# Router logits with their operands swapped, a last eviction shared by two engines, a drain moved, and a new order planned with later landings

## The chip, the cores and the metric

The kernel runs on one core of one Trainium2 chip. The metric is the device time of one execution in microseconds (us), the median of several executions. The core has five engines with queues of their own, each worked off in order: TensorE (PE; its weight loads are shown as PEld), VectorE (DVE), ScalarE (ACT), GpSimd (POOL) and SyncE (SP), which here issues nearly all transfers. The indirect gathers and scatters are issued by GpSimd.

## The reference

Three blocks follow one another.

1. Attention over 32 memories for 4 batches, 8 heads, 576 positions, 64 wide. `a` is the softmax of `phi` over the positions; `k_m` and `v_m` are the sums of k and v weighted with `a`; the scores of q against `k_m` go through a softmax over the 32 memories and weigh `v_m`.
2. A gated layer on 2304 tokens of 512: `silu(x @ w_gate) * (x @ w_val) @ w_out`, 1536 wide.
3. A mixture of 8 experts with one expert a token:

```
logits = x @ w_gate                      # 2304 x 8
expert_idx = argmax(logits)
gate_w = softmax(logits)[expert_idx]
h = relu(disp @ w1[e]);  y = h @ w2[e]   # 512 -> 1024 -> 512
out[i] = gate_w[i] * y[expert_idx[i], pos[i]]
```

A token is kept while its expert has counted fewer than `capacity` tokens before it.

## The kernel before

Matmuls run on pairs of fp32r tiles: a value is cut into a rounded high part and the rest (`cut`, L430 and L432: a ScalarE copy, then a subtraction on VectorE or GpSimd), and three of the four products of parts are summed.

Batches 0 and 1 are the first pair, 2 and 3 the second. Per batch, `phi` is turned and the memories are formed (L523, L545), turned again (L584), and q is multiplied with them for the scores (L632), whose softmax runs on VectorE, GpSimd and ScalarE. `memories_in` projects the memories through the gate and value weights (pm, L838), and the result is cut into mh on ScalarE and VectorE. `batch` multiplies it with the attention weights (pg, pv, L940); `gates` applies silu. `products` multiplies with the output weights (py, L984), in three groups G of four 128-wide slices. The weights are converted once on chip, stored in DRAM, and reloaded for the second pair (L807).

After the third group each chunk of 128 tokens leaves as `rows`. `rows_out` turns it with four transposes (pw, L1033), cuts it into yh, and multiplies it with the router weights rg, 16 columns (8 experts, high and low parts), in eight matmuls (pl, L1043). There are 18 chunks. `route` takes three at a time, six blocks in all: it copies pl from 16 partitions to SBUF (lt, L1082, ScalarE), turns it back with three transposes so that tokens stand on partitions (L1086), and computes the choice, the position and the gate with some thirty small VectorE instructions.

The experts run as units of up to 288 tokens. A unit's index list feeds three indirect gathers (L1452, GpSimd), the rows are turned (L1473), and `up` and `down` multiply with the expert's w1 and w2 (L1500, L1540). The weights come in eight transfers of 512 KB a unit and are cut on ScalarE and VectorE (`part1`, `part2`). Each quarter of the result is copied out (y, L1555, ScalarE), turned (po, L1566), scaled with the gate on VectorE (L1579) and scattered to the output (L289, GpSimd). Two early units need only the first pair, six come later, then one unit of 128 tokens (class `Small`), whose result is scaled in one VectorE instruction (L1733) and scattered last. A GpSimd drain (L1639) stands behind the gather of this last unit.

No engine chooses its order at run time. A planner, `Loom`, runs in Python while the program is built. Every piece of work is a generator that says which engine it needs next, for how long, and which events and buffers it waits for; the planner keeps a clock for each engine and takes the waiting piece with the lowest rank among those that could start. The ranks are the numbers in `RANK`, added to due times. A transfer is given a time of landing, `loom.landed`: one after another at 410 KB a us, and 0.75 us on top. Instructions go into each engine's queue in the order that the planner comes to them. On the chip each waits for its semaphores only, but it holds everything behind it on its engine.

Of the kernel before, what the change touches and what calls it, by code (L numbers as in the profile page):

```python
# [21 lines left out]
RANK = {  # L22
    "gate": -318.1, "mh": -66.7, "mem": -464.3, "mem0": 36.2, "py": 408.0, "out": -17.0, "tables": 252.9, "warm": -9,
# [5 lines left out]
    "mh1": -406.0, "py1": 7.4, "turn": -21.0, "route": -340.6, "zeros": -518.5, "lists": -509.6, "marks": -304.6, "pick": -568.4,  # L29
# [149 lines left out]
def on_pe(count, n=288, passes=1):  # L179
    return "PE", count * (passes * n / 2400 + 0.011)  # L180
# [18 lines left out]
def attention_moe_moe_kernel(  # L199
# [60 lines left out]
    def t2k(shape, name, dt=F32):  # L260
        return sb.tile(shape, dt, tag="t2k", name=name, bufs=4)
# [172 lines left out]
    class Attention:  # L434
# [12 lines left out]
        def load(self):  # L447
            b = self.b
            if b >= 2:
                for Q in range(2):  # L450
                    yield atts[b - 1].kvq[Q][1]
            yield raw_s
            self.ph = traw([128, 2, S], "ph")
            loom.set(self.ph_in)
            for Q in range(2):
                yield on_dma(295)
                nc.sync.dma_start(self.ph[:, Q], phi[b, Q])
                loom.set(self.phq[Q], loom.landed)
# [7 lines left out]
        def load_kv(self, Q):  # L466
            slot = self.kv_slot(Q)
            if slot is not raw_s:
                for hp in range(2):
                    yield slot  # L470
            else:
                yield self.ph_in
                yield pair
                for hp in range(2):
                    yield raw_s
                loom.put(pair)
            for hp in range(2):
                raw = self.raws[Q][hp] = kvraw(self.b, Q).rearrange("p (t h) j d -> p t h j d", t=2)
                yield on_dma(655)
                nc.sync.dma_start(raw, kv[self.b, Q, hp])  # L480
                loom.set(self.kvq[Q][hp], loom.landed)
# [4 lines left out]
        def load_q(self, n):  # L486
# [20 lines left out]
            loom.set(self.qq[n], loom.landed)  # L507
# [285 lines left out]
    def reload(key, k):  # L793
# [15 lines left out]
        loom.set(wdone[1, key], loom.landed)  # L809
# [207 lines left out]
    def rows_out(P, py, rows, k):  # L1017
# [23 lines left out]
        for d in range(NDT):  # L1041
            for a in range(2):
                nc.tensor.matmul(  # L1043
                    pl[: 2 * E, c * TC : (c + 1) * TC],
                    rg[:, d].rearrange("p a e -> p (a e)"),
                    yh[:, a, d * TC : (d + 1) * TC],
                    start=(d == 0 and a == 0),
                    stop=(d == NDT - 1 and a == 1),
                )
# [24 lines left out]
    def route(blk):  # L1074
# [4 lines left out]
        yield t2k_s  # L1079
        lt = t2k([2 * E, RB * TC], "lt")  # L1080
        yield on_a(RB * TC)
        nc.scalar.copy(lt, pl[: 2 * E, : RB * TC])  # L1082
        px = pl[:, RB * TC :]
        yield on_pe(RB, 130)
        for c in range(RB):
            nc.tensor.transpose(  # L1086
                px[:, c * 2 * E : (c + 1) * 2 * E], lt[:, c * TC : (c + 1) * TC], ident[: 2 * E, : 2 * E]
            )
        loom.put(t2k_s)
        lg2 = small([TC, RB, 2, E], "lg2")  # L1090
        yield on_v(48)
        nc.vector.tensor_copy(lg2, px[:, : RB * 2 * E].rearrange("p (c a e) -> p c a e", a=2, e=E))
# [30 lines left out]
        pp = pl[:, RB * TC + 64 :]  # L1123
# [255 lines left out]
    class Unit:  # L1379
# [19 lines left out]
        def loads(self):  # L1399
# [4 lines left out]
            for d in range(NDT):  # L1404
# [5 lines left out]
                loom.spawn(self.part1(d, raw), self.base - 8 + d + RANK["w1"], loom.landed)  # L1410
            for t in range(NF2 // 2):
# [7 lines left out]
                loom.spawn(self.part2(t, raw), self.base + 8 + t + RANK["w2"], loom.landed)  # L1419
# [133 lines left out]
        def column(self, d, p2, y2):  # L1553
# [19 lines left out]
            for c in range(NC):  # L1573
# [17 lines left out]
                if c % 2 or c == NC - 1:  # L1591
                    loom.put(raw_s)
            loom.put(gw_s)
# [5 lines left out]
    class Small(Unit):  # L1599
# [20 lines left out]
        def gather(self):  # L1620
# [18 lines left out]
            nc.gpsimd.drain()  # L1639
# [69 lines left out]

        def down(self):  # L1710
            yield self.base + 6 + RANK["down"]
# [20 lines left out]
            yield on_v(DM)  # L1732
            nc.vector.tensor_scalar(ot, p2, self.gw, None, ALU.mult)  # L1733
# [122 lines left out]
```

## Time and profile before

| | us |
|---|---|
| median of three runs | 693.19 (692.75 to 693.77) |
| profiled execution, its own time | 699.14 |
| its span, first to last instruction | 697.4 |
| TensorE matmuls busy | 658.2 |
| VectorE, ScalarE, GpSimd busy | 407.9, 388.9, 232.2 |
| mean granted TensorE clock | 0.978 |

The durations all come from the one profiled execution, 5.95 us slower than the median of the runs. Busy times of a TensorE row overlap: matmuls are pipelined, and what one costs is read from the distance between starts, not from its own duration. In rows of the order of time, the number in brackets is the idle time of the engine before the instruction, with what ended it. The granted clock is given as a share: 1.00 is 2.4 GHz, 0.5 is 1.2 GHz, and a number between is a mean over a stretch with both.

### The profile page before, as it was taken

The numbers are of one execution on the slowest core, as the hardware profiler recorded it, in microseconds if no ns is written. First come the engines' busy times: TensorE is split into PE (matmuls) and PEld (weight loads), VectorE is DVE, ScalarE is ACT, GpSimd is POOL, SyncE is SP. The second block draws the span as 40 slices with busy tenths as digits, with TensorE's granted clock in tenths as the row PEclk, the third lists the DMA queues.
The fourth block names the chain that finished last, engine by engine and source line by source line (L and its number), as shares of the span: only waits on it lengthen the run. The fifth ranks groups of instructions, "written<-read, shape, count | busy, mean of one in ns | idle before, by whom it ended". The sixth has DMA issues, their size and how long they took to land. (4 is left out here: it accounts for less than half of the span.)

```text
span 697.4 us, 12482 instructions
## 1 busy us (share of the span) xinstructions
PE 658.2 (94%) x4681; PEld 604.5 (87%) x4681; DVE 407.9 (58%) x899; ACT 388.9 (56%) x735; POOL 232.2 (33%) x230
## 2 busy tenths in 40 slices
PE   6699999999898999999999999999999999999995
PEld 5489998988787788889988988898998999999983
DVE  3887744867566567603634646864573754754552
ACT  4779998986666356725713733434364544643450
POOL 1657654534434302511401320023461521321202
PEclk9699999999989999999999999999999999999997
DMA  9995768767743215794331432343964846655251
GB/s 349 402 378 194 257 229 297 288 220 253 293 175 133 89 57 195 265 290 143 128 121 37 176 105 107 107 123 88 259 205 140 274 123 205 198 152 203 85 192 36
DMA packets 48736, 132.03 MB, mean 189 GB/s; under 512 B 7648, under 2 KB 16864, under 8 KB 44064
## 3 DMA queue, kind: packets, MB, share of 16 engines
q1 hardware_dynamic: 45440, 121.44, 50.7%
q0 software_dynamic: 3232, 9.74, 4.2%
q8 instruction: 39, 0.64, 0.4%
q14 instruction: 25, 0.20, 0.1%
HBM read 98.10 MB, written 33.33 MB: 188 GB/s over the span
## 5 line engine op out<-in xcount | busy, mean ns | idle before, releaser
L984 PE MATMUL py<-wo,gh 128*128 128x512 f32 x648 | 156.7, 393 | 0.0
L984 PEld LDWEIGHTS py<-wo,gh 128*128 128x128 f32 x648 | 118.8, 188 | 23.3 <-ACT gh L430 0.2
L432 POOL TENSOR_TENSOR gh<-sg,gh 128x288 fp32r<-128x288 f32 x96 | 78.9, 826 | 151.6 <-ACT gh L430 151.1
L1540 PE MATMUL p<-hh,w2h 128*128 128x288 f32 x768 | 113.9, 299 | 0.0
L1500 PE MATMUL p<-xt,w1h 128*128 128x288 f32 x768 | 110.5, 297 | 0.0
L1540 PEld LDWEIGHTS p<-hh,w2h 128*128 128x128 f32 x768 | 104.3, 189 | 0.3 <-DVE hh L1516 0.2
L1500 PEld LDWEIGHTS p<-xt,w1h 128*128 128x128 f32 x768 | 104.0, 188 | 0.3 <-DVE yh L432 0.2
L289 POOL DMA_INDIRECT out_dram<-ot,idx x24 | 48.9, 2036 | 146.7 <-DVE ot L1579 143.7
L940 PE MATMUL pg<-at,mh 128*128 128x288 f32 x576 | 95.3, 303 | 2.3 <-DVE mh L432 1.2
L940 PE MATMUL pv<-at,mh 128*128 128x288 f32 x576 | 92.7, 298 | 0.9 <-ACT sg L850 0.9
L940 PEld LDWEIGHTS pg<-at,mh 128*128 128x128 f32 x576 | 82.9, 191 | 7.6 <-issue 2.3
L940 PEld LDWEIGHTS pv<-at,mh 128*128 128x128 f32 x576 | 82.1, 190 | 2.4 <-ACT sg L850 1.4
L853 DVE SCALAR_TENSOR_TENSOR sg<-sg,pv 128x288 f32<-128x288 f32 x96 | 43.1, 452 | 63.7 <-ACT sg L850 39.4
L432 DVE TENSOR_TENSOR mh<-pm,mh 64x512 fp32r<-64x512 f32 (+1 forms) x88 | 60.4, 686 | 18.5 <-ACT mh L430 16.2
L1514 ACT ACTIVATE hh<-p 128x288 fp32r<-128x288 f32 x64 | 26.2, 410 | 69.0 <-PE p L1500 60.7
L1516 DVE SCALAR_TENSOR_TENSOR hh<-p,hh 128x288 fp32r<-128x288 f32 x64 | 28.6, 450 | 56.0 <-ACT hh L1514 55.1
L430 ACT ACTIVATE mh<-pm 64x512 fp32r<-64x512 f32 (+1 forms) x88 | 51.9, 591 | 14.3 <-PE pv L940 9.2
L432 DVE TENSOR_TENSOR w2h<-w2r,w2h 128x1024 fp32r<-128x1024 f32 x34 | 41.3, 1216 | 28.2 <-ACT w2h L430 27.9
L430 ACT ACTIVATE gh<-sg 128x288 fp32r<-128x288 f32 x96 | 42.0, 441 | 26.8 <-DVE sg L853 25.5
L850 ACT ACTIVATE sg<-pg 128x288 f32<-128x288 f32 x96 | 38.6, 407 | 28.8 <-PE pg L940 26.1
L838 PE MATMUL pm<-wgv,tv 128*128 128x256 f32 x336 | 50.3, 301 | 4.3 <-DVE mh L432 2.2
L838 PEld LDWEIGHTS pm<-wgv,tv 128*128 128x128 f32 x336 | 46.9, 207 | 7.3 <-DVE mh L432 2.6
(215 smaller groups left out, 838.2 us busy)
## 6 DMA issues: line engine op xcount, KB each, us to landing
w1r<-in_moe_w_dram SPq DMA_DIRECT2D x36, 512.0 KB
w2r<-in_moe_w_dram SPq DMA_DIRECT2D x36, 512.0 KB
wr<-in_moe_w_gv_dram SPq DMA_DIRECT2D x24, 512.0 KB
wsc<-wgv SPq DMA_DIRECT2D x12, 1024.0 KB
wgv<-wsc SPq DMA_DIRECT2D x12, 1024.0 KB
kvraw<-in_kv_dram SPq DMA_DIRECT2D x16, 640.0 KB
wr<-in_moe_w_out_dram SPq DMA_DIRECT2D x12, 512.0 KB
osc<-wo SPq DMA_DIRECT2D x6, 1024.0 KB
```

Of the source, the lines that this page charges most:

```text
L289: ins = nc.gpsimd.indirect_dma_start(*args, **kwargs)
L430: nc.scalar.activation(hi, src, AF.Copy)
L432: (nc.gpsimd if pool else nc.vector).tensor_sub(lo, src, hi.bitcast(F32))
L838: nc.tensor.matmul(pm[:, Q * 256 : (Q + 1) * 256], tv[:, 2 * Q + hp, a, :], w[:, c, 2 * Q + hp], start=(k == 0 and n3 == 0), stop=(k == le ...
L850: nc.scalar.activation(sg, pg[:, :NB], AF.Silu, scale=1.0 / 256)
L853: nc.vector.scalar_tensor_tensor(sg, sg, 2.0**-16, pv[:, :NB], ALU.mult, ALU.mult)
L940: nc.tensor.matmul(pg[:, :NB], mh[:, a, Q, gv * 128 : gv * 128 + 128], at[:, Q, c, ns], start=(Q == 0 and n3 == 0), stop=(Q == 1 and n3 == 2),
L984: nc.tensor.matmul(py, gh[:, a, k * TC : (k + 1) * TC], wtiles[P, ws[j // 2]][:, j % 2, c, :], start=(j == 0 and n3 == 0), stop=(j == FG - ...
L1500: nc.tensor.matmul(p1[:, :NB], self.w1[d][:, a, f * 128 : f * 128 + 128], self.xt[d][:, c], start=(d == 0 and n3 == 0), stop=(d == NDT - 1 ...
L1514: nc.scalar.activation(dst[:, 0], p1[:, :NB], AF.Relu)
L1516: nc.vector.scalar_tensor_tensor(dst[:, 1], p1[:, :NB], 0.0, dst[:, 0].bitcast(F32), ALU.max, ALU.subtract)
L1540: nc.tensor.matmul(p2[:, :NB], self.w2[f // 2][:, f % 2, a, d * 128 : d * 128 + 128], self.hh[f][:, c], start=(f == 0 and n3 == 0), stop=( ...
```

## The change

- Logits: stationary and moving operand are swapped. Now yh (128 columns) is loaded and rg (16 columns) streams, so that the result has tokens on partitions. The copy lt and the transposes back are gone from `route`, with their buffer; the rest of `route` reads pl at other columns.
- `Small.down`: the last eviction is done half by ScalarE (new function `half`), half by VectorE; the scatter waits for both.
- The drain moves from behind the last unit's gather to behind the scatters of unit 6 of 0 to 7.
- The planner takes the loads of phi, kv and q of batches 2 and 3 and the reloads of converted weights to land 1.0 us later, and the experts' weights 1.5 us later.
- All ranks are new, and two settings of the planner: `slack` 0.02 to 0.01 and `look` 5.0 to 4.9.

```diff
-    "gate": -318.1, "mh": -66.7, "mem": -464.3, "mem0": 36.2, "py": 408.0, "out": -17.0, "tables": 252.9, "warm": -9,
+    "gate": -511.5, "mh": -86.7, "mem": -582.5, "mem0": -16.4, "py": 288.4, "out": -483.7, "tables": 87.1, "warm": -9,
...
-                loom.set(self.phq[Q], loom.landed)
+                loom.set(self.phq[Q], loom.landed + (1.0 if self.b >= 2 else 0.0))
...
-                loom.set(self.kvq[Q][hp], loom.landed)
+                loom.set(self.kvq[Q][hp], loom.landed + (1.0 if self.b >= 2 else 0.0))
...
-            loom.set(self.qq[n], loom.landed)
+            loom.set(self.qq[n], loom.landed + (1.0 if self.b >= 2 else 0.0))
...
-        loom.set(wdone[1, key], loom.landed)
+        loom.set(wdone[1, key], loom.landed + 1.0)
...
                 nc.tensor.matmul(
-                    pl[: 2 * E, c * TC : (c + 1) * TC],
+                    pl[:, c * 2 * E : (c + 1) * 2 * E],
+                    yh[:, a, d * TC : (d + 1) * TC],
                     rg[:, d].rearrange("p a e -> p (a e)"),
-                    yh[:, a, d * TC : (d + 1) * TC],
...
-        yield t2k_s
-        lt = t2k([2 * E, RB * TC], "lt")
-        yield on_a(RB * TC)
-        nc.scalar.copy(lt, pl[: 2 * E, : RB * TC])
-        px = pl[:, RB * TC :]
-        yield on_pe(RB, 130)
-        for c in range(RB):
-            nc.tensor.transpose(
-                px[:, c * 2 * E : (c + 1) * 2 * E], lt[:, c * TC : (c + 1) * TC], ident[: 2 * E, : 2 * E]
-            )
-        loom.put(t2k_s)
...
-        nc.vector.tensor_copy(lg2, px[:, : RB * 2 * E].rearrange("p (c a e) -> p c a e", a=2, e=E))
+        nc.vector.tensor_copy(lg2, pl[:, : RB * 2 * E].rearrange("p (c a e) -> p c a e", a=2, e=E))
...
-                loom.spawn(self.part1(d, raw), self.base - 8 + d + RANK["w1"], loom.landed)
+                loom.spawn(self.part1(d, raw), self.base - 8 + d + RANK["w1"], loom.landed + 1.5)
...
-                loom.spawn(self.part2(t, raw), self.base + 8 + t + RANK["w2"], loom.landed)
+                loom.spawn(self.part2(t, raw), self.base + 8 + t + RANK["w2"], loom.landed + 1.5)
...
+            if self.n == NEARLY + NSTAT - 2:
+                nc.gpsimd.drain()
             loom.put(gw_s)
...
-            nc.gpsimd.drain()
...
+        def half(self, dst, src):
+            yield on_a(DM // 2)
+            nc.scalar.activation(dst, src, AF.Copy, scale=self.gw)
+            loom.set(self.halved)
...
-            yield on_v(DM)
-            nc.vector.tensor_scalar(ot, p2, self.gw, None, ALU.mult)
+            h = DM // 2
+            loom.spawn(self.half(ot[:, :h], p2[:, :h]), self.rank_of_end)
+            yield on_v(h)
+            nc.vector.tensor_scalar(ot[:, h:], p2[:, h:], self.gw, None, ALU.mult)
+            yield self.halved
```

## Rows read from the trace of the kernel before

**Rows 1.** The page's busy times: us, share of the span, instructions.

```profile
PE 658.2 (94%) x4681; PEld 604.5 (87%) x4681; DVE 407.9 (58%) x899; ACT 388.9 (56%) x735; POOL 232.2 (33%) x230
```

**Rows 2.** Stage table: length, busy time by engine, granted clock, DMA share, GB/s.

```profile
0.00:40.00 40.00, 27.16 (x224) 21.77 (x225) 26.09 (x61) 25.89 (x51) 15.77 (x21) 0.83 0.97 381
...
188.00:224.00 36.00, 29.34 (x184) 26.43 (x183) 22.13 (x42) 23.38 (x45) 17.73 (x18) 0.86 0.44 176
224.00:300.00 76.00, 73.27 (x509) 63.66 (x509) 50.14 (x172) 42.21 (x77) 24.63 (x27) 1.00 0.46 158
...
470.00:662.00 192.00, 186.85 (x1439) 185.34 (x1437) 106.84 (x161) 90.99 (x160) 60.69 (x37) 1.00 0.57 176
662.00:697.40 35.40, 25.90 (x142) 21.74 (x142) 13.80 (x14) 11.06 (x15) 5.60 (x5) 0.90 0.32 117
```

**Rows 3.** TensorE in order of time, 188 to 224: start, length, what.

```profile
191.89 2.13 PE L632 MATMUL psc<-qt,tk 128*64 128x288 f32 x8 [2.93 <-DMA qt<-in_q_dram]
...
203.80 0.54 PE L940 MATMUL pg<-at,mh 128*128 128x288 f32 x2 [0.71 <-ACT mh L430]
...
209.61 1.19 PE L632 MATMUL psc<-qt,tk 128*64 128x288 f32 x8
...
219.56 1.65 PE L838 MATMUL pm<-wgv,tv 128*128 128x256 f32 x6 [2.21 <-DVE mh L432]
```

**Rows 4.** SyncE's queue in order of time: the issue of that q.

```profile
183.33 0.33 SPq L506 DMA_DIRECT2D qt<-in_q_dram  x1
```

**Rows 5.** Stage table behind the first hole.

```profile
193.90:198.20 4.30, 4.30 (x31) 4.24 (x30) 2.12 (x6) 2.27 (x6) 1.16 (x1) 0.82 0.38 160
```

**Rows 6.** TensorE in order of time, around routing blocks at 247 and 436.

```profile
246.90 0.18 PE L1126 MATMUL pl<-ohb,tri 128*128 128x8 bf16 x1
...
246.98 0.17 PE L1129 MATMUL pl<-ohb,onesb 128*128 128x8 bf16 x1
...
435.95 0.35 PE L1086 MATMUL pl<-ident,lt 16*128 16x16 f32 x3
436.23 0.65 PE L1043 MATMUL pl<-yh,rg 128*16 128x128 f32 x8
436.73 1.04 PE L1033 MATMUL pw<-ident,rows 128*128 128x128 f32 x8
```

**Rows 7.** Two lines' weight loads: shortest, median, longest ns; first and last start.

```profile
L1043 PEld LDWEIGHTS pl<-yh,rg x144: 92/95/100, 231.0 to 445.0; 128*16 128x16 f32 x144
...
L940 PEld LDWEIGHTS pg<-at,mh x576: 186/188/333, 36.6 to 403.1; 128*128 128x128 f32 x192
```

**Rows 8.** Groups by line: the copy in `route`; busy us, mean ns, idle.

```profile
L1082 ACT COPY lt<-pl 16x384 f32<-16x384 f32 x6 | 2.8, 466 | 11.6 <-PE pl L1043 11.6
```

**Rows 9.** The line of the drain: ns, start.

```profile
L1639 POOLq DRAIN  x1: 6924/6924/6924, 577.5 to 577.5; - x1
```

**Rows 10.** GpSimd in order of time: the last large unit's first scatter.

```profile
682.08 0.92 POOL L289 DMA_INDIRECT out_dram<-ot,idx  x1 [18.26 <-DVE ot L1579]
```

**Rows 11.** Groups by line, shapes apart: evictions of 256 and 512 columns.

```profile
L1022 DVE TENSOR_TENSOR rows<-py,yp 128x256 f32<-128x256 f32 x4 | 1.5, 420 | 3.4 <-PE py L984 3.4
L1011 ACT COPY yp<-py 128x256 f32<-128x256 f32 x4 | 1.4, 378 | 3.0 <-PE py L984 3.0
...
L1733 DVE TENSOR_SCALAR ot<-p,gw_s 128x512 f32<-128x512 f32 x1 | 0.8, 751 | 3.6 <-PE p L1721 3.6
```

**Rows 12.** TensorE and ScalarE in order of time, around 493 and 665.

```profile
492.74 1.06 ACT L430 ACTIVATE w1h<-w1r 128x1024 fp32r<-128x1024 f32 x1 [1.60 <-DMA w1r<-in_moe_w_dram]
...
494.14 0.53 PE L1566 MATMUL po<-ident,y 128*96 128x128 f32 x3 [0.99 <-ACT y L1555]
...
664.30 1.06 ACT L430 ACTIVATE w1h<-w1r 128x1024 fp32r<-128x1024 f32 x1 [1.26 <-DVE w1h L432]
...
665.70 0.53 PE L1566 MATMUL po<-ident,y 128*96 128x128 f32 x3 [1.63 <-ACT y L1555]
```

**Rows 13.** Groups by line: the transposes of a unit's result; idle before them.

```profile
L1566 PE MATMUL po<-ident,y 128*96 128x128 f32 x96 | 15.9, 275 | 6.4 <-ACT y L1555 4.7 <-issue 1.7
```

More of the change, by code (lines that the diff above doesn't have):

```diff
@@ L22 @@
 RANK = {
-    "gate": -318.1, "mh": -66.7, "mem": -464.3, "mem0": 36.2, "py": 408.0, "out": -17.0, "tables": 252.9, "warm": -9,
[5 rows of a table removed]
-    "mh1": -406.0, "py1": 7.4, "turn": -21.0, "route": -340.6, "zeros": -518.5, "lists": -509.6, "marks": -304.6, "pick": -568.4,
[3 rows of a table removed]
+    "gate": -511.5, "mh": -86.7, "mem": -582.5, "mem0": -16.4, "py": 288.4, "out": -483.7, "tables": 87.1, "warm": -9,
[5 rows of a table added]
+    "mh1": -518.0, "py1": 86.7, "turn": -430.3, "route": 181.9, "zeros": -31.3, "lists": -569.1, "marks": -465.0, "pick": -422.3,
[3 rows of a table added]
 }
@@ L1122, in route @@
         nc.vector.tensor_copy(ohj, ohb[:, 2 * RB - 1].unsqueeze(2).to_broadcast([TC, E, JU]))
-        pp = pl[:, RB * TC + 64 :]
+        pp = pl[:, 64:]
         flat = ohb.rearrange("p c e -> p (c e)")
@@ L1708, in hidden @@
                 loom.set(self.h_ready[f])
+        def half(self, dst, src):
+            yield on_a(DM // 2)
+            nc.scalar.activation(dst, src, AF.Copy, scale=self.gw)
+            loom.set(self.halved)
         def down(self):
-            yield self.base + 6 + RANK["down"]
+            self.rank_of_end, self.halved = self.base + 6 + RANK["down"], Event()
+            yield self.rank_of_end
             yield self.h_ready[0]
```

16 rows, old and new, of the table RANK are left out of this document.

## The prediction

> **What bounds the kernel now.** I read four views in this order: the busy times, the stage table, TensorE's order of time in two stages, and the groups by line. TensorE does matmuls for 658.2 of 697.4 us [rows 1], so only what touches its queue counts, and the reader is to see in the stage table where it does not run. In 0 to 40 it lacks 12.8 us at a clock of 0.83, with the DMA engines 97% taken; in 188 to 224 6.7 us at 0.86; in 224 to 300 2.7; in 470 to 662 5.2; in the last stretch 9.5, mostly after its last product [rows 2]. Between the two bad stages, and from 300 to 430, nothing is to be had but fewer TensorE instructions. The rest of the engines are at 56 to 58% or less and matter by the order of their queues.
>
> In 188 to 224 there are three kinds of hole. At 191.89 the scores of the second pair waited 2.93 us for q, issued at 183.33: 8.6 us for 576 KB. At 203.80 and 219.56 products waited 0.71 and 2.21 us for cuts of mh on ScalarE and VectorE [rows 3, 4]. Each hole is followed by work at the lower clock: eight score matmuls take 2.13 us after the first hole and 1.19 us at 209.61 [rows 3], and 193.9 to 198.2 runs at a mean of 0.82 [rows 5]. With 1.00 for 2.4 GHz and 0.5 for 1.2 GHz, a mean of 0.86 over 36 us is 5.0 us of full-speed work lost. So this stage holds 6.7 + 5.0 = 11.7 us.
>
> **Router logits.** The 144 logits products swap operands: 16 columns of weights under 128 moving ones become 128 columns of weights (yh) under 16 moving ones. Now eight of them occupy 0.50 us (436.23 to 436.73), 62 ns each, set by the 128 moving columns, and their 16-column loads take 95 ns in the record; an fp32r load of 128 columns takes 188 ns [rows 6, 7]. The difference, 93 ns for 112 columns, is 0.83 ns a column, so 128 columns need 106 ns of loading. Under 288 moving columns that hides; under 16 there is nothing to hide it but the next load. Eight take 0.85 us, 0.35 more than now, and 18 groups 6.3 us more. Removed are 18 transposes in six groups of three, 0.28 us each (435.95 to 436.23), 1.7 us [rows 6]. Net +4.6 us, on the path, since these groups stand at 228 to 268 and 424 to 445, where TensorE has almost no idle time [rows 2]. Lower end: loads as quick as the bf16 ones, four starts in 0.08 us, 27 ns each [rows 6], give 18 x (0.22 - 0.50) - 1.7 = -6.8 us. Upper end: 188 ns each with no overlap, 18 x (1.50 - 0.50) - 1.7 = +16.4. The transposes removed also had 128-column loads under 16 columns, at 93 ns; that would be +2.7. I take 106 because it is worked out from loads of the same type and shape.
>
> The Trainium skill ("TensorE: Matmul & The Clock Gate", section "LDWEIGHTS (loading the stationary operand)") says that a load costs its columns divided by 1.2 per ns, whatever the rows, which speaks against this edit: 107 ns for 128 columns, and a sum of +4.7 us as an estimate from that page. The trace's 0.83 ns a column agrees; that the load then sets the pitch is shown by no row here.
>
> The six copies of lt on ScalarE (466 ns each, 2.8 us) go too [rows 8]. ScalarE is 56% busy and off the path there: nothing. The routing chain gets shorter by a copy and a transpose, but its end feeds gathers for units that come behind the two early ones, and TensorE has their work meanwhile: nothing. Should the cover be gone, one hop of about 0.5 us a block would show, 3 us.
>
> **Drain.** It lasted 6.92 us on GpSimd [rows 9]. It moves behind the scatters of the seventh unit, the last but one of the large ones, after which GpSimd stood idle for 18.26 us until 682.08 [rows 10]. Behind it wait the last unit's three scatters; 18.26 - 6.92 leaves 11 us. Nothing. If that idle time shrank below 6.92, each us less would delay the tail by one.
>
> **Last rows.** 512 columns on VectorE took 751 ns; 256 columns take 420 on VectorE and 378 on ScalarE, side by side [rows 11]. This is on the path: only the scatter and the end of the program follow. ScalarE has nothing left to do then. Gain 0.33 us; at best 0.37, and a loss of up to 0.2 if ScalarE wakes that much later.
>
> **Later landings and the new order.** These change no instruction but the order on every queue, and with it which wait is met. The second pair's loads are priced 1.0 us later, the experts' rows 1.5, reloads 1.0. Three terms:
> - Second pair. The hole named by a transfer costs 2.93 idle, 0.94 in the score matmuls and 0.18 x 4.3 = 0.77 behind them: 4.6 us [rows 3, 5]. Ends: 0 to -11.7 if all three holes close, and +4.6 if a second such hole opens at another of the q loads. I take -4.6: other products fill this hole and those made by cuts stay. The later price of reloads and of kv takes nothing, since no TensorE wait here is put down to them; at worst a product placed late leaves one more hole of 2.21.
> - Expert units. At 494.14 and 665.70 TensorE waited 0.99 and 1.63 us for the copy of y; ScalarE had taken a cut of w1h first, which itself stood 1.60 us for its rows at 492.74 and began 1.26 us late, behind VectorE's cut, at 664.30 [rows 12]. Its queue is in order, so a cut placed too early holds the copy. A price 1.5 us later puts the copy first. I take those two, -2.6; ends 0 and the 6.4 of all such holes [rows 13], or the same 6.4 more if copies fall behind cuts of w2h.
> - Everything else. The start could move either way; with the DMA engines at 97% I take 0, with 4 us (a third of its 12.8) on both sides.
>
> **Sum.** +4.6 - 0.33 - 4.6 - 2.6 = -2.9 us. The profiled execution took 699.14 us, so its successor should take 696.2; the three runs have a median of 693.19, 5.95 lower, and the same difference there gives 690.3.
>
> **Rivals.** About 0.2%, 1.4 us, is what a measurement of this kernel can tell from no change.
> 1. The slow loads with nothing to pay for them: slower. The place is the 18 groups of logits, the price +4.6 with nothing won by the order. For: the pitch there is set by the longer of two streams, and the holes made by cuts have nothing to do with landings. Against: two kinds of hole are clearly a matter of order. It decides when the new order takes back less than 4.3 us. 693.19 + 4.6 - 0.33 = 697.5. Chance 0.27.
> 2. The change does not do what it says: one us does not cover 2.93. Then q is awaited 1.0 us less, the clock still falls, the units give 2.6: +4.6 - 0.33 - 1.0 - 2.6 = +0.7, 693.9. For: a transfer that took 8.6 us. Chance 0.17.
> 3. Quick loads. If an fp32r load can go at the bf16 pitch, the router gives -6.8 and all the rest stays: -14.3, 678.9. Against it stands 188 ns for the fp32r load [rows 7]. The Trainium skill (same page, section "Weight-path perf modes") turns the fast load on for 128 weights of a type that is not FP32, and whether fp32r counts as that it does not say. Chance 0.09.
> 4. The whole second-pair stage and all holes of the units close: -11.7 - 6.4 + 4.6 - 0.33 = -13.8, 679.4. For: they are what a better order can reach. Against: the cuts of mh share two engines with gates and scores. Chance 0.09.
> The forecast, with its own range of 687 to 693, has 0.38.
>
> **How the numbers follow.** Faster by over 0.2%: rivals 3 and 4 (0.18) and 0.35 of the forecast's 0.38, 0.53. Within 0.2%: 0.03 of the forecast and 0.14 of rival 2, 0.17. Slower: rival 1 and 0.03 of rival 2, 0.30. The range from 682.0 to 698.5 leaves out most of rivals 3 and 4 below and some 0.07 of rival 1 above, where the unknown load pitch or a new hole adds to it.
>
> **What would show it.** Logits loads at 188 ns and eight of them in about 0.85 us up to the next group; 0.5 or less proves that step wrong, 1.5 the upper end. No hole before the second pair's first scores, and a clock above 0.86 in that stage. Copies of y ahead of cuts of w1h on ScalarE, and less than 4 us of idle before the transposes of po. The drain ending ahead of the last unit's first scatter. Two half evictions of about 0.4 us at the end. The prediction is wrong in its reasons if the time moves by what happens in 0 to 40, or if new holes outweigh those that close.

## The result, and the profile after

The changed kernel takes 687.0 us, the median of five runs (686.65 to 689.26), where the kernel before beside it takes 693.19 (692.75 to 694.2): a ratio of 0.9917, with an interval of 0.9893 to 0.9941. That is 6.2 us less. The forecast was 690.3, 2.9 us less. The profiled execution of after took 689.26 us, at the upper end of its runs; that of before took 699.14, 5 us above its own. The difference of the two traces, 9.9 us, is therefore larger than that of the kernels, and a second trace of before is among the experiments.

The page of after, busy times (us, share, instructions), answers to [rows 1]:

```profile
PE 661.3 (96%) x4663; PEld 612.5 (89%) x4663; DVE 408.8 (59%) x899; ACT 382.1 (56%) x726; POOL 227.6 (33%) x230
```

TensorE idles 26.2 us instead of 39.2, but is busy 3.1 us longer, with 18 instructions fewer. Where that lies is in the stage table of after (length; busy time of PE, PEld, DVE, ACT, POOL; granted clock; DMA share; GB/s), beside [rows 2]:

```profile
0.00:40.00 40.00, 27.88 (x215) 21.22 (x216) 26.81 (x60) 25.97 (x52) 15.60 (x21) 0.79 0.96 379
...
188.00:224.00 36.00, 34.77 (x252) 30.29 (x250) 18.33 (x38) 18.41 (x38) 13.16 (x14) 1.00 0.55 200
224.00:300.00 76.00, 74.15 (x486) 67.64 (x483) 52.89 (x177) 42.84 (x77) 26.87 (x29) 0.93 0.44 148
...
470.00:662.00 192.00, 188.60 (x1444) 187.75 (x1444) 112.62 (x166) 95.32 (x164) 58.48 (x37) 0.99 0.60 192
```

Three things are to be seen. From 188 to 224 the idle time fell from 6.7 to 1.2 us and the clock rose from 0.86 to 1.00. From 224 to 300 the clock fell from 1.00 to 0.93, which over 76 us is 5.3 us of full-speed work. From 470 to 662 the idle time fell from 5.2 to 3.4.

TensorE in order of time at the start of the second pair (start, length, what, idle time before and what ended it), beside [rows 3]:

```profile
192.12 1.29 PE L545 MATMUL kvp<-kvraw,ex 112*32 112x128 f32 x20 [0.97 <-DMA kvraw<-in_kv_dram]
193.67 1.29 PE L545 MATMUL kvp<-kvraw,ex 112*32 112x128 f32 x20 [0.26 <-DMA kvraw<-in_kv_dram]
...
201.44 1.19 PE L632 MATMUL psc<-qt,tk 128*64 128x288 f32 x8
```

The scores come at 201.44 instead of 191.89, with other products ahead of them, do not wait for q, and take 1.19 us instead of 2.13. What is left is 1.23 us for kv. The holes of 0.71 and 2.21 us for mh are gone too.

TensorE in order of time at a chunk's logits, first in before, then in after, and the loads of that line in after, beside [rows 6, 7]:

```profile
412.79 0.64 PE L1043 MATMUL pl<-yh,rg 128*16 128x128 f32 x8
413.27 1.12 PE L1033 MATMUL pw<-ident,rows 128*128 128x128 f32 x8
```

```profile
408.66 0.95 PE L1043 MATMUL pl<-rg,yh 128*128 128x16 f32 x8
409.46 1.09 PE L1033 MATMUL pw<-ident,rows 128*128 128x128 f32 x8
```

```profile
L1043 PEld LDWEIGHTS pl<-rg,yh x144: 186/192/338, 213.4 to 441.1; 128*128 128x128 f32 x144
```

Eight products now occupy 0.80 us, 100 ns each on the average, against 0.48 here and 0.50 in the group of [rows 6].

The new loss of clock begins in the routing. TensorE in order of time there, and the stage table behind it:

```profile
254.67 1.15 PE L1043 MATMUL pl<-rg,yh 128*128 128x16 f32 x7 [1.10 <-DVE yh L432]
...
259.06 1.71 PE L1043 MATMUL pl<-rg,yh 128*128 128x16 f32 x8
```

```profile
250.00:255.00 5.00, 3.47 (x28) 3.26 (x28) 4.76 (x19) 2.87 (x4) 1.16 (x1) 1.00 1.02 416
255.00:260.00 5.00, 5.00 (x29) 4.97 (x28) 4.56 (x16) 2.59 (x6) 2.28 (x2) 0.53 0.03 10
260.00:265.00 5.00, 5.00 (x23) 5.00 (x24) 4.08 (x18) 4.72 (x7) 2.17 (x2) 0.50 0.00 0
```

TensorE waits 1.10 us for yh with one of eight products issued, and the 10 us behind it run at about half speed, with no further hole: some 4.9 us.

The end of after, ScalarE, VectorE and GpSimd in order of time, beside [rows 11]:

```profile
681.13 0.47 ACT L1702 ACTIVATE ot<-p,gw_s 128x256 f32<-128x256 f32 x1 [3.39 <-PE p L1717]
681.64 0.48 DVE L1731 TENSOR_SCALAR ot<-p,gw_s 128x256 f32<-128x256 f32 x1 [2.52 <-ACT ot L1702]
682.40 1.02 POOL L289 DMA_INDIRECT out_dram<-ot,idx_s  x1 [2.08 <-DVE ot L1731]
```

VectorE's half begins when ScalarE's is done. From the first half to the scatter it is 1.27 us.

The drain, beside [rows 9, 10], by the view of its line and GpSimd's order of time:

```profile
L1583 POOLq DRAIN  x1: 9986/9986/9986, 651.4 to 651.4; - x1
```

```profile
674.72 0.92 POOL L289 DMA_INDIRECT out_dram<-ot,idx  x1 [21.46 <-DVE ot L1568]
```

It takes 10.0 us instead of 6.9, from 651.4 to 661.4. The next scatter comes at 674.72, after GpSimd has stood idle for 21.46 us; 13.3 of these lie behind the drain.

### The profile page after: what moved, and what is told of

Same layout as the page of the kernel before. It is cut to its first block, busy times and chain, and to the rows that moved or that the text cites. A ratio compares the mean times of both kernels' runs of the same rounds, so it can differ in the third digit from the quotient of the medians.

```text
span 687.5 us, 12456 instructions
## 1 busy us (share of the span) xinstructions
PE 661.3 (96%) x4663; PEld 612.5 (89%) x4663; DVE 408.8 (59%) x899; ACT 382.1 (56%) x726; POOL 227.6 (33%) x230
## 5 line engine op out<-in xcount | busy, mean ns | idle before, releaser
L1529 PEld LDWEIGHTS p<-hh,w2h 128*128 128x128 f32 x768 | 105.8, 191 | 1.3 <-DVE hh L1505 1.3
L289 POOL DMA_INDIRECT out_dram<-ot,idx x24 | 44.2, 1840 | 139.2 <-DVE ot L1568 134.1
L432 DVE TENSOR_TENSOR w1h<-w1r,w1h 128x1024 fp32r<-128x1024 f32 x36 | 43.4, 1218 | 23.2 <-ACT w1h L430 23.2
L850 ACT ACTIVATE sg<-pg 128x288 f32<-128x288 f32 x96 | 38.5, 407 | 26.2 <-PE pg L940 22.2
```

The source lines that it names most:

```text
L289: ins = nc.gpsimd.indirect_dma_start(*args, **kwargs)
L432: (nc.gpsimd if pool else nc.vector).tensor_sub(lo, src, hi.bitcast(F32))
L850: nc.scalar.activation(sg, pg[:, :NB], AF.Silu, scale=1.0 / 256)
L1529: nc.tensor.matmul(p2[:, :NB], self.w2[f // 2][:, f % 2, a, d * 128 : d * 128 + 128], self.hh[f][:, c], start=(f == 0 and n3 == 0), stop=( ...
```

## Experiments

Each run has its own runs of the kernel before on the same chip, and ratios are to these. I first asked what the logits cost and why, then which part of the order brings the gain.

### Logits: is it the load that sets the pitch?

`half_products`: four products a chunk instead of eight, in after's order; the low part of yh is left out of the logits.

```diff
-            for a in range(2):
+            for a in range(1):
...
```

> The kernel after, with the same order on every engine, but only four of the eight logits products of a chunk: the low part of yh is left out of the logits (72 of 144 products and their weight loads go). Theory A (a 128-column fp32r load sets the pitch at 100 ns and TensorE is the path there): each chunk loses 4 x 0.10 us, 18 chunks 7.2 us, so about 7 us faster than the kernel after, more if the clock no longer falls around 255. Theory B (the loads hide, the products cost their 60 ns or less, or the path is elsewhere): 0 to 4 us faster.

`moving128`: the same loads of yh, but rg streamed eight times over, so that 128 columns move instead of 16. The result takes eight times the columns in PSUM, of which `route` reads the first copy.

```diff
...
-                    rg[:, d].rearrange("p a e -> p (a e)"),
+                    rg[:, d].rearrange("p a e -> p (a e)").unsqueeze(1).to_broadcast([128, 8, 2 * E]),
...
```

> The kernel after, same order, but the 16 router columns are streamed eight times (128 moving columns under the same 128-column loads). Theory A (the load sets the pitch, 100 ns for eight in 0.80 us, and 53 ns of streaming hides under it): eight products still take about 0.80 to 0.9 us and the time stays that of the kernel after within 1.5 us. Theory B (the pitch is the stream plus the load, one after the other): 100 + 47 ns, eight in 1.18 us, 18 chunks 6.8 us slower. Theory C (a fixed cost of a product, independent of either): no change at all, 0.80 us to the digit.

Measured: 681.19 us, 0.9749 (0.9711 to 0.9787), and 690.16 us, 0.9867 (0.9824 to 0.991), where the kernel with after's order on that chip (`end_two_banks`, below) has 691.33. TensorE in order of time at one chunk, first of `half_products`, then of `moving128`:

```profile
402.85 0.51 PE L1043 MATMUL pl<-rg,yh 128*128 128x16 f32 x4
403.21 1.24 PE L1033 MATMUL pw<-ident,rows 128*128 128x128 f32 x8
```

```profile
407.15 1.00 PE L1043 MATMUL pl<-rg,yh 128*128 128x128 f32 x8
407.99 1.06 PE L1033 MATMUL pw<-ident,rows 128*128 128x128 f32 x8
```

Half of the products take 0.36 us instead of 0.80, and eight times the moving columns take 0.84: the moving side is nearly free. Nor is it a fixed cost of a product: with 128 moving columns in both, eight take 0.48 us in before, where 16 columns are loaded, and 0.84 here, where 128 are. So the load sets the pitch. Four products fewer are 0.44 us less, which makes it 110 ns for 128 fp32r columns; the 0.80 us are less than eight times that, since a group's first load costs less. The Trainium skill ("TensorE: Matmul & The Clock Gate", section "LDWEIGHTS (loading the stationary operand)") gives columns divided by 1.2 per ns, an estimate of 107 ns; the runs agree within 3 ns.

Half the products take 18 x 0.44 = 7.9 us away, and the whole kernel gets 10.1 us shorter on that chip. The rest fits the clock of 224 to 300, 1.00 instead of 0.93 (5.3 us), less the idle time there, which grew from 1.8 to 4.3 us: 10.7 together. In `moving128` that clock is 1.00 too, although TensorE waits for yh at the same place:

```profile
254.76 0.99 PE L1043 MATMUL pl<-rg,yh 128*128 128x128 f32 x7 [1.00 <-DVE yh L432]
```

So a hole of nearly the same length was followed by half clock with 16 columns and by none with 128; whether the columns or the 0.10 us of hole decide isn't settled. The kernel as a whole is only 1.2 us below `end_two_banks`. Its profiled execution, 2.1 us above its median, has a hole of 3.63 us in the unit stage, at 518.34, for a copy of y that itself stood 4.46 us on ScalarE for what the trace calls remote, none of the core's engines; whether the other executions have it isn't known.

### The last rows: why one half after the other?

`end_two_banks`: the last products go to two tiles of 256 columns in two PSUM banks, twice as many products of half the columns.

```diff
+                    for px, sl in ((p2, slice(0, h)), (p3, slice(h, DM))):
...
-            nc.vector.tensor_scalar(ot[:, h:], p2[:, h:], self.gw, None, ALU.mult)
+            nc.vector.tensor_scalar(ot[:, h:], p3[:, :h], self.gw, None, ALU.mult)
```

> The kernel after, same order, but the last unit's second product goes into two PSUM banks of 256 columns, so that VectorE's half waits for TensorE alone. Theory A (the two halves run one after the other in the kernel after because both read one bank): the halves start within 0.1 us of each other, from the first half's start to the scatter 1.27 us becomes about 0.8; 24 products of 512 columns become 48 of 256, at 119 instead of 117 ns per 256 columns, no cost to speak of. Gain about 0.5 us, below what the times can tell; the trace decides. Theory B (they share something else, as the tile they write): they still run one after the other, no gain.

Measured: 691.33 us, 0.9901 (0.9868 to 0.9935). Its end, in order of time:

```profile
681.24 0.47 ACT L1702 ACTIVATE ot<-p,gw_s 128x256 f32<-128x256 f32 x1 [3.35 <-PE p L1721]
681.36 0.48 DVE L1735 TENSOR_SCALAR ot<-p,gw_s 128x256 f32<-128x256 f32 x1 [2.09 <-PE p L1721]
682.63 1.02 POOL L289 DMA_INDIRECT out_dram<-ot,idx_s  x1 [2.17 <-DVEq L1802]
```

From two banks the halves run side by side, although both still write one tile, ot; so in after it is the shared p2, one bank, that makes VectorE wait. By the trace this is a wait for ScalarE's half [2.52 <-ACT ot L1702], that is for a semaphore in the program as built; whether the chip would have run the two side by side from one bank is not shown. The time expected up to the scatter, 0.8 us, did not come: it starts 0.79 us behind the later half, where it was 0.28 before and in after, and the whole takes 1.39 us. Why it starts so late I did not settle.

### The drain, and before's code in the new order

`after_old_drain` puts the drain back behind the last unit's gather.

```diff
-            if self.n == NEARLY + NSTAT - 2:
-                nc.gpsimd.drain()
...
             loom.set(self.gathered, loom.now + SWDGE_LANDING)
+            nc.gpsimd.drain()
```

> The kernel after with the drain put back behind the gather of the last unit; the order on every engine is the same but for the drain itself. Theory A (the drain is hidden in idle time of GpSimd at either place): within 0.2% of the kernel after, about 0.990 to 0.992 of the kernel before. Theory B (at its late place it delays the last scatters, or at its early place a gather): 1 to 6 us apart from the kernel after.

Measured: 687.47 us, 0.9916 (0.9888 to 0.9944): the move costs and brings nothing.

`old_code_new_order` is before's code, with the old logits, eviction and drain, planned with the new ranks and settings and the later landings (that of q is shown).

```diff
-RANK = { ... before ... }
+RANK = { ... after ... }
...
-            loom.set(self.qq[n], loom.landed)
+            loom.set(self.qq[n], loom.landed + (1.0 if self.b >= 2 else 0.0))
...
```

> The code of the kernel before (logits with the weights' 16 columns, transposes back, one eviction, early drain) planned with the new ranks, settings and later landings. Theory A (the order brings all of the gain and the swap of the router costs about 4 us of TensorE): faster than the kernel after by 2 to 6 us, 681 to 685, with the second-pair stage 188 to 224 free of large holes as in the kernel after. Theory B (the swap of the router brings the gain by a shorter chain): near the kernel before, 690 to 693. The order is not quite that of the kernel after, since the planner sees other work, so new holes of 1 to 3 us may blur it.

Measured: 687.92 us, 0.9841 (0.9803 to 0.9879). The order alone brings more than the whole change, and in this pair the new code takes some of it back.

### Code, ranks, landings: all eight combinations

`new_code_old_order` is the new code with the ranks and landings of before; `after_no_land` is after without the later landings (that of q is shown); `before_land` is before with the later landings alone. The two settings of the planner go with the ranks throughout.

```diff
...
-            loom.set(self.qq[n], loom.landed + (1.0 if self.b >= 2 else 0.0))
+            loom.set(self.qq[n], loom.landed)
...
```

> The code of the kernel after (swapped logits, last rows by two engines, late drain) planned with the old ranks, settings and landings. Theory A (the swap costs 0.32 us a chunk and saves 0.28 us a block, +4.0 us in all, the last rows +0.24): 3 to 6 us slower than the kernel before, more where the clock falls in the routing stretch. Theory B (the swap gains by a shorter chain): 1 us or more faster than the kernel before. The order is not quite that of the kernel before, so holes of 1 to 2 us either way may blur it.

> The kernel after, same ranks, but the planner takes all loads to land at the time it computes, without the 1.0 and 1.5 us. Theory A (the gain is that of the later landings: copies and scores are put behind what really lands late): the hole before the second pair's first product and holes before po come back, 3 to 6 us slower than the kernel after, 0.996 to 1.000 of the kernel before. Theory B (the gain is that of the new ranks, the landings alone do little): within 2 us of the kernel after.

> The kernel before, old ranks, with the later landings alone. Theory A (the later landings carry the gain): 3 to 6 us faster than the kernel before, with less idle time before po and before the second pair's scores. Theory B (landings work only with ranks sought for them): within 2 us of the kernel before, or slower, since its ranks were sought for the other landings.

The last two combinations followed: `old_code_new_rank_no_land`, with before's code, and `new_code_old_rank_land`, with the code of after.

> The code of before, planned with the ranks of after and without the later landings. Measured so far, as ratios to before: old code with new ranks and landings 0.984, old code with old ranks and landings 0.986, new code with new ranks and no landings 0.985, new code with old ranks and no landings 1.000. Theory A (ranks and landings are two ways to the same gain, some 10 us from the holes before the second pair's scores and the clock of the stage behind them): 0.980 to 0.990, 679 to 686 us beside a before of 693, with no hole over 0.5 us before the second pair's first scores. Theory B (the new ranks help only with the code that they were found for): 0.995 to 1.005. Theory C (any other plan than that of before gives about -1 per cent, by chance): cannot be told from A here; the run of the kernel with new code, old ranks and landings tells it.

> The code of after, planned with the ranks of before and with the later landings. Theory A (the landings alone close the holes before the second pair's scores, whatever the code): 0.984 to 0.992 of before, 682 to 688 us, and PE busy at least 33.5 of 36 us in 188 to 224 us against 29.9 for the same code and ranks without the landings. Theory B (landings help only with the ranks or the code of before): 0.996 to 1.004 and the holes at 193 and 219 us as in the kernel without them.

| ranks, landings | before's code | after's code |
|---|---|---|
| old, old | 1 (692.96) | 1.0003 [0.9971, 1.0034] (694.23) |
| old, later | 0.9862 [0.9808, 0.9917] (684.85) | 0.9895 [0.9857, 0.9934] (686.16) |
| new, old | 0.9876 [0.984, 0.9913] (685.5) | 0.9847 [0.9789, 0.9906] (683.6) |
| new, later | 0.9841 [0.9803, 0.9879] (687.92) | 0.9917 [0.9893, 0.9941] (687.0) |

Medians in us stand in round brackets; that of old code, new ranks and later landings was taken beside a before of 698.67. Either the ranks or the landings alone bring 1.1 to 1.5%, and both together 1.6% with before's code. With the new code both together bring less than the ranks alone: the two intervals overlap (0.9893 to 0.9906), but on one chip after's order (`after_old_drain`) took 685.94 to 689.17 us and `after_no_land` 681.29 to 684.89. New code against old, row by row, is +0.03, +0.33, -0.29 and +0.76%, a mean of +0.2% or 1.4 us, which these intervals do not tell from nothing. Which of the three landings (attention, reloads, experts) counts, no run separates.

Theory A of the last two runs holds, and B falls. The three before them missed: `after_no_land` was to be 3 to 6 us slower than after, or within 2, and came faster; `before_land` gained more than the 3 to 6 us (8.1 by the medians); `new_code_old_order` was to be 3 us slower or 1 faster, and is level. Against "any other plan gains by chance" stands only this last one, also a new plan, which keeps the holes and gains nothing. The line 188:224 of the stage tables of `new_code_old_order`, `before_land`, `old_code_new_rank_no_land`, `new_code_old_rank_land` and `after_no_land`, in this order, with later stages of the first and the last:

```profile
188.00:224.00 36.00, 29.90 (x204) 27.31 (x204) 24.25 (x45) 26.53 (x51) 19.18 (x20) 0.95 0.52 201
224.00:300.00 76.00, 75.30 (x502) 67.23 (x501) 49.98 (x172) 39.95 (x73) 24.44 (x27) 1.00 0.48 159
300.00:470.00 170.00, 169.10 (x1108) 155.44 (x1107) 90.47 (x245) 71.44 (x144) 30.18 (x35) 1.00 0.40 131
```

```profile
188.00:224.00 36.00, 34.04 (x233) 29.51 (x230) 23.14 (x44) 22.36 (x45) 16.03 (x17) 1.00 0.52 200
```

```profile
188.00:224.00 36.00, 35.53 (x249) 31.78 (x248) 23.54 (x44) 24.82 (x50) 16.76 (x18) 1.00 0.50 180
```

```profile
188.00:224.00 36.00, 34.33 (x224) 29.89 (x225) 22.23 (x41) 22.65 (x43) 15.98 (x17) 1.00 0.44 164
```

```profile
188.00:224.00 36.00, 36.00 (x250) 32.48 (x249) 23.51 (x43) 24.65 (x50) 16.73 (x18) 1.00 0.50 181
224.00:300.00 76.00, 73.28 (x482) 65.84 (x481) 51.73 (x173) 38.36 (x72) 25.63 (x29) 0.98 0.47 159
```

The one that gains nothing is busy 29.9 us at 0.95; those that gain are busy 34.0 to 36.0 us at 1.00. No other stage parts them so, and `old_code_new_order`, which gains too, is busy 34.4 us at 1.00. What they share is that the second pair's first scores come later: at 199.34, 195.67, 196.32 and 195.76, against 193.27 in the one that waits:

```profile
193.27 1.19 PE L632 MATMUL psc<-qt,tk 128*64 128x288 f32 x8 [2.37 <-DMA qt<-in_q_dram]
```

A q issued at 185.27 there and at 185.32 in `after_no_land` is waited for 2.37 us in the first and not at all in the second.

### Before once more, and a version that beats both

`before_again` is the kernel before, unchanged, for a second trace.

> The kernel before, once more, for a second trace. Theory A (the holes of the second pair and of the unit stage, and the clock of 0.86 behind the first, belong to its plan): holes of 2 to 3 us at 192 to 194 us and over 2 us at 219 us, PE busy 29 to 30.5 of 36 us in 188 to 224 us, holes of about 1 us each before the two po transposes at 494 and 666 us, ratio 0.998 to 1.002. Theory B (they vary from run to run): any of them gone or a third of its size, and PE busy over 32 us in 188 to 224 us.

Measured: 692.13 us, 0.9988 (0.9959 to 1.0017); the profiled execution took 691.73. Its stage table, and TensorE's order of time at the holes:

```profile
188.00:224.00 36.00, 29.68 (x202) 27.00 (x201) 23.86 (x45) 26.23 (x52) 18.55 (x19) 0.95 0.51 198
224.00:300.00 76.00, 73.20 (x509) 63.59 (x508) 49.10 (x171) 40.51 (x74) 24.55 (x27) 1.00 0.47 158
300.00:470.00 170.00, 168.30 (x1126) 153.14 (x1125) 90.75 (x247) 73.10 (x148) 31.11 (x36) 1.00 0.41 131
470.00:662.00 192.00, 188.27 (x1453) 187.27 (x1452) 110.19 (x162) 93.91 (x163) 62.57 (x35) 1.00 0.58 184
```

```profile
192.45 1.19 PE L632 MATMUL psc<-qt,tk 128*64 128x288 f32 x8 [2.27 <-DMA qt<-in_q_dram]
...
204.43 1.33 PE L940 MATMUL pg<-at,mh 128*128 128x288 f32 x4 [0.82 <-DVE mh L432]
...
218.80 0.98 PE L838 MATMUL pm<-wgv,tv 128*128 128x256 f32 x6 [2.21 <-DVE mh L432]
...
490.73 0.53 PE L1566 MATMUL po<-ident,y 128*96 128x128 f32 x3 [1.18 <-ACT y L1555]
...
660.10 0.53 PE L1566 MATMUL po<-ident,y 128*96 128x128 f32 x3 [2.10 <-ACT y L1555]
...
680.34 3.29 PE L1721 MATMUL p<-w2h,hh 128*128 128x512 f32 x12 [0.69 <-ACT hh L430]
```

The holes that the prediction named belong to the plan: all are there again, for q 2.27 us, for mh 1.02 (at 203.08), 0.82 and 2.21, for y 1.18 and 2.10. The clock does not: 0.95 instead of 0.86, and 1.19 us for the score products behind the same hole. The first trace of before has these besides, in the order of time:

```profile
474.96 0.53 PE L1566 MATMUL po<-ident,y 128*96 128x128 f32 x3 [1.60 <-ACT y L1555]
...
524.80 0.53 PE L1566 MATMUL po<-ident,y 128*96 128x128 f32 x3 [1.71 <-issue]
...
686.05 4.86 PE L1721 MATMUL p<-w2h,hh 128*128 128x512 f32 x12 [0.69 <-ACT hh L430]
```

What made it 7.4 us longer is the clock (0.09 x 36 = 3.2 us), these two holes with the 0.99 us at 494.14 (4.3 instead of 1.2) and the last twelve products (4.86 us instead of 3.29): 7.9 together.

`no_land_end_dve` is `after_no_land` with the last 512 columns evicted by VectorE in one instruction, as before.

```diff
-            nc.scalar.activation(dst, src, AF.Copy, scale=self.gw)
...
-            nc.vector.tensor_scalar(ot[:, h:], p2[:, h:], self.gw, None, ALU.mult)
+            nc.vector.tensor_scalar(ot, p2, self.gw, None, ALU.mult)
```

> The code of after with the ranks of after and no later landings, and the last 512 columns evicted by VectorE in one instruction instead of two halves. The order of PE is otherwise that of the kernel without later landings, which measured 683.6 us (0.985). Theory A (the two halves run one after the other, so that they cost 1.27 us up to the scatter against 1.03 for the one): 0.2 us less, 683.4 us, not to be told by the median, but by the end of the trace: 1.0 to 1.1 us from the start of the eviction to the last scatter. Theory B (the one instruction costs what it saves elsewhere): 1.2 to 1.4 us there.

Measured: 683.15 us, 0.9839 (0.9801 to 0.9876), the lowest median of the kernels that leave nothing out, though by its ratio level with `after_no_land` (0.9847) and `old_code_new_order` (0.9841). Its interval lies wholly below that of after. The end of it, in order of time:

```profile
676.08 0.75 DVE L1730 TENSOR_SCALAR ot<-p,gw_s 128x512 f32<-128x512 f32 x1 [2.00 <-PE p L1716]
677.11 1.01 POOL L289 DMA_INDIRECT out_dram<-ot,idx_s  x1 [1.83 <-DVEq L1796]
```

One instruction reaches the scatter in 1.03 us, the two halves of after in 1.27. Theory A, by the trace; the medians can't show 0.24 us.

## Why the prediction was right and where it was wrong

**The time.** 687.0 lies in the range and on the side that was forecast, 3.3 us below the number. The order brought more than I gave it, and the sum was right in sign because of that. That it came so near was in part luck: the 2.6 us of the units did not come, a clock fall of 5.3 us was not in the sum, and the second pair, which gave 2.3 more than forecast, made up for only a part of these.

**Router logits, forecast +4.6: right in mechanism and near in size.** The pitch is 110 ns, not 106; eight take 0.80 us instead of 0.85. Against the 0.48 us of most groups of before, 18 x 0.32 - 1.7 = +4.0 us of TensorE time. Neither end (27 ns and 188 ns a load) came. What the step lacked is that the slower logits stand in the stretch where a wait of 1.10 us was followed by half clock: 5 us more, in after, `after_old_drain` and `end_two_banks` alike, which share the order (0.93 over 224 to 300 in each). Over the four pairs of the table the new code costs 1.4 us, less than the 4.0. The step took all of it to lie on the path; the stage tables say that most of the rest went into idle time. From 224 to 470 TensorE idles 4.5 us in the second trace of before and 1.6 in `new_code_old_order`, the new code planned with the same ranks and landings; in the other three pairs it is 5.2 and 2.1, 4.8 and 3.1, 5.4 and 2.3. That is 2.7 us in the mean, and leaves 1.3.

**Second pair, forecast -4.6: the term that was mis-sized.** I let the hole for q close and left those for mh in place. All three went, and the clock with them: 11.7 us were lost there in the first trace of before, 8.1 in the second (6.3 idle and 0.05 x 36), 1.2 in after. That is 6.9 to 10.5, not 4.6, and of the two I take 6.9, since the second trace is near the median of its kernel. The error has two parts. Holes that cuts of mh make were a matter of the order as well, which the end of -11.7 in my bounds allowed; and a granted clock of one execution was entered as if it belonged to the kernel. The reason given, that the later landings do it, holds only half: ranks alone do it too.

**Expert units, forecast -2.6: not shown.** The hole at 494.14 is gone, the last one stands (1.63 us in the first trace of before, 2.10 in the second). TensorE in order of time in after:

```profile
652.89 2.15 PE L1529 MATMUL p<-hh,w2h 128*128 128x288 f32 x14 [1.06 <-DVE hh L1505]
656.92 0.53 PE L1555 MATMUL po<-ident,y 128*96 128x128 f32 x3 [1.88 <-ACT y L1544]
```

In after it has 1.88 us, and a new one of 1.06 stands ahead of it. From the first up product to the last scatter it is 251.5 us in the first trace of before (440.46 to 691.98), 246.1 in the second (438.57 to 684.71) and 246.4 in after (435.99 to 682.40). So this stage gives nothing against a middling execution, as far as one trace of each tells; what I read there as a hole of the plan was partly one of the run. The step that failed is that the later price puts the copy of y first. ScalarE in order of time at the last hole in after:

```profile
655.52 1.06 ACT L430 ACTIVATE w1h<-w1r 128x1024 fp32r<-128x1024 f32 x1 [3.01 <-DMA w1r<-in_moe_w_dram]
656.48 0.38 ACT L1544 COPY y<-p 128x288 f32<-128x288 f32 x1
```

The cut of w1h still stands ahead of the copy, and now waits 3.01 us for its rows.

**Last rows, forecast -0.33: wrong in sign, +0.24.** I took "side by side" from two evictions of before that stand in the same rows [rows 11]. They belong to different groups G, ScalarE's to the first and VectorE's to the third, and no row there has two engines on one tile. From one bank the built program makes the one wait for the other.

**Drain, forecast 0: right.** Its 10.0 us end 13.3 us ahead of the next scatter, and `after_old_drain` is level with after. **Everything else, forecast 0:** the idle time of 0 to 40 went from 12.8 to 12.1.

**The sum again.** From the second trace of before to that of after: +4.0 (logits), -6.9 (second pair), +5.3 (clock in the routing) less 0.9 of idle time there, 0 (units), +0.24, -0.4 (0 to 40), and -1.8 of idle time in 40 to 188 and 300 to 470 (2.36 to 0.52) make -0.5 us, where the traces differ by 2.5: 2 us have no place. The medians differ by 6.2: after's profiled execution was 2.3 us above its median, that of the second trace 0.4 below its own, and before's median was 1.1 lower there than beside after (692.13, 693.19). The account thus gives the signs and the order of the parts, not the median to a microsecond. The clock fall is no matter of one execution: the three traces of after's order with unchanged logits have it. It is the likely reason why ranks and landings together bring less with the new code than the ranks alone. On one chip the mean granted clock of nine runs of `after_old_drain` has a median of 0.982, that of four of `after_no_land` 0.9855, which is 0.0035 of 687 or 2.4 us; by the traces, 0.93 against 0.98 over 76 us is 3.8. With the 1.2 us for kv that only after has, less 0.9 of idle time behind it, these 3.8 make 4.1, where the medians on that chip differ by 3.9 (687.47, 683.6). No run took only that fall away.

Of the rivals, the first (slow loads, nothing from the order) describes `new_code_old_order` in its mechanism, but that came at 1.0003 and not at +4.3 us. The second (one us does not cover the wait for q) falls, since that hole is gone, with the later landings and without. The third (quick loads) falls by the 110 ns. Of the fourth the first half came true, the whole second-pair stage, and the other half, the holes of the units, did not.

## What to carry to other kernels

Before pricing holes and clock falls from one trace, take a second of the same kernel: holes that repeat belong to the plan, a clock fall behind them may not. When operands are swapped so that few columns move, price the product by its load. And when a plan is searched anew together with a change of code, run the code with the old plan and the plan with the old code: here the plan brought all of the gain.

## What was not expected of the hardware

- Two engines reading halves of one PSUM bank ran one after the other (681.13 and 681.64); from two banks they began 0.12 us apart. The wait is for a semaphore that the built program has there; what the chip would do without it is not shown.
- A load of 128 fp32r columns is recorded as 192 ns, but one more load costs 110 ns; the length of a record is no pitch.
- Behind a hole of 1.10 us the clock stayed near 0.5 for 10 us, in three runs of one order; with 128 moving columns instead of 16, behind 1.00 us at the same place, it stayed at 1.00.
